# Small expert blocks: the first product in column halves, with TensorE's loop code at another offset and fewer row copies

## The chip, the cores and the metric

The kernel runs on one core of one Trainium2 chip. The metric is device microseconds of one execution, as the median of several runs; lower is better. A core has five engines with queues of their own: TensorE (PE in the profile, with its weight loads as PEld), VectorE (DVE), ScalarE (ACT), GpSimd (POOL) and SyncE (SP), which here issues most DMAs.

## What is computed

Sigmoid attention over 8 batches, 12 heads, 448 positions and 64 columns a head, all in float32, and then a mixture of 8 experts over the 3584 rows of 768 that attention leaves. Cut to what matters:

```python
def _moe_ref(x, w_skip, w_gate, w1, w2):          # x: 3584 x 768
    skip_score = x @ w_skip
    do_compute = skip_score > 0
    out = x.copy()
    xc = x[do_compute]
    logits = xc @ w_gate                          # 8 experts
    e_idx = np.argmax(logits, axis=1)
    ...                                           # gate_w: softmax weight of the chosen expert
    for e in range(E):
        mask = e_idx == e
        h = np.maximum(xc[mask] @ w1[e], 0.0)     # w1[e]: 768 x 1024
        y[mask] = gate_w[mask, None] * (h @ w2[e])  # w2[e]: 1024 x 768
    out[do_compute] = xc + y
    return out
```

## The kernel before, in words

**Attention** takes the first 272 us or so. Each batch's rows are routed as soon as its attention is done: every row that is computed gets a record (its gate and its row number) in a list of its expert. Attention's output is stored to the result, and the experts add to it.

**Two blocks of 128 rows** of the largest expert are then written out by hand, while VectorE plans the rest: a table `slots` says block by block which rows come, what kind of block it is, and which expert's weights are to be loaded behind it.

**The loop** at line 1553 runs over the rest of the blocks, 14 of them here. `choose` reads one word of `slots` and takes one of four arms:

- `FULL` and `SPLIT` (function `block`): 128 rows. Weights and rows are split into a high and a low part (`wh`, `wl`, `xh`, `xl`, type fp32r), and each product is the sum of three. `SPLIT` also makes the split weights of the next expert on ScalarE and VectorE.
- `HALF`: up to 64 rows, plain float32 weights as they were loaded (`raw1`, `raw2`), the array in two column groups of 64 (`side`).
- `FEW`: up to 32 rows, plain float32, four column groups of 32 (`quarter`).

`HALF` and `FEW` are the small blocks, and both have the same parts. The rows lie turned (columns of the row on the partitions) in `xf`, one piece of 128 for each j in range(6). The **first product** multiplies them with `raw1`, 768 x 1024, and leaves its result in PSUM: in `FEW` the 1024 columns lie as four groups of 256 on 32 partitions each, in `HALF` as two of 512 on 64. **relu** copies it to `hs` (ScalarE; two pieces of 128 columns in `FEW`, pieces of 128, 128 and 256 in `HALF`). TensorE **turns** `hs` piece by piece against the identity into PSUM, ScalarE copies the turned pieces to `ht`, and the **second product** multiplies `ht` with `raw2` into `py`. In `FEW` its terms go in the order j = 0, 2, 1, 3, and piece j % 2 of `ht` is what a term needs: the first half of the terms needs the first piece alone.

Between the first product and the turns of `hs`, TensorE also turns the next block's rows (`turn_x`, six turns of 128 x 128 into `pxt`), SP gets the four loads of the next expert's `raw1` (`load_w1`), and POOL the row gather for the block after the next (`fetch`). Behind the turns of `hs`, `ready_x` makes `xh` (`hi_x`, ScalarE), `xf` (`whole_x`, ScalarE: 64 of each 128 columns) and `xl` (`lo_x`, VectorE). `put` scatters the block's result to the output by a DMA on POOL that adds.

The order of the instructions on each engine is the order in the code (`tc.manual_schedule()`); waits between engines are put in by the framework, from what each instruction writes and reads. `ph`, `py` and `pht` are PSUM tiles that all arms share. `ph[0]`, `ph[1]`, `pht[0]` and `pht[1]` are four banks.

[...]

Of the kernel before, what the change touches and what calls it, by code (L numbers as in the profile page):

```python
# [14 lines left out]
AF = mybir.ActivationFunctionType  # L15
# [4 lines left out]
P = 128  # L20
# [3 lines left out]
def kernel(  # L24
# [11 lines left out]
    nc = tc.nc  # L36
# [11 lines left out]
    NK1 = DM // P  # L48
    NK2 = FF // P
    H1 = FF // 2  # L50
# [6 lines left out]
    SM = 32  # L57
# [15 lines left out]
    ident = const.tile([P, P], F32, name="ident")  # L73
# [613 lines left out]
    for n, (b, hp) in enumerate(steps):  # L687
# [39 lines left out]
        for c in range(4):  # L727
            at = wk.tile([P, 2, S], F32, tag="A", name=f"at_{b}_{hp}_{c}", bufs=5)
# [125 lines left out]
    ph = new_ph(0)  # L854
# [13 lines left out]
    xf = rows_pool.tile([P, NK1, MD], F32, name="xf")  # L868
    ys = rows_pool.tile([P, DM], F32, name="ys")
    ht = rows_pool.tile([P, 4 * P], F32, name="ht")  # L870
    hs = rows_pool.tile([P, FF], F32, name="hs")
# [202 lines left out]
    ph = new_ph(1)  # L1074
# [38 lines left out]
    def whole_x(h, pieces):  # L1113
        for s in pieces:
            n = s.stop - s.start
            nc.scalar.activation(
                xf[:, 3 * h + s.start : 3 * h + s.stop, :],
                pxt[h][:, s.start * P : s.stop * P].rearrange(
                    "p (j t) -> p j t", j=n
                )[:, :, :MD],  # L1120
                AF.Copy,
            )

    def ready_x():
        for h in range(2):
            hi_x(h, pxt[h], xh)
        for h in range(2):
            whole_x(h, [slice(j, j + 1) for j in range(3)])
        for h in range(2):
            lo_x(h, pxt[h], xh, xl)  # L1130

# [23 lines left out]
    for j in range(2):  # L1155
        gemm2(j, hh0, hl0, py)
    turn0(1)
    nc.tensor.addr_align(bass.FETCH_BLOCK_INSTRUCTIONS, offset=0, max_nops=0)
    for j in range(2, NK2 - 3):
        gemm2(j, hh0, hl0, py)  # L1160
    pxt = [ps_b.tile([P, 512], F32, tag="b", name="pxt0"), new_t("pxt1")]
# [1 line left out]
        turn_x(xc, h, pxt[h])  # L1163
        hi_x(h, pxt[h], xh)
    for h in range(2):
        whole_x(h, [slice(j, j + 1) for j in range(3)])
    for h in range(2):
        lo_x(h, pxt[h], xh, xl)
    for j in range(NK2 - 3, NK2):
# [52 lines left out]
    raw1 = [[raw1g[h, i // 3][:, i % 3, :] for h in range(2)] for i in range(NK1)]  # L1222
    raw2 = [raw2g[j // 2][:, j % 2, :] for j in range(NK2)]

    ph = [new_t(f"ph{h}") for h in range(2)]
    py = new_s("py")
    pht2 = new_s("pht")
    pht = [pht2[:, h, :] for h in range(2)]

    def next_expert(word):  # L1230
        return word & (NE - 1), (word & (2 * NE)) >> (2 * NE).bit_length() - 1
# [176 lines left out]
    def few(i, word):  # L1408

        nx = next_expert(word)  # L1410
        for o in range(2):
            nc.vector.tensor_copy(gate2[o * SM : (o + 1) * SM], recs[:SM, 0, 0:1])  # L1412
        take_rec()

        def quarter(dst, g, n, a, w, j, most):
            nc.tensor.matmul(  # L1416
                dst[g * SM : (g + 1) * SM, :n],
                a,
                w,
                start=(j == 0),  # L1420
                stop=(j == most - 1),
                tile_position=(0, g * SM),
            )

        Q1 = FF // 4
        for j in range(NK1):
            for g in range(4):
                s = slice((g % 2) * Q1, (g % 2 + 1) * Q1)
                quarter(ph[0], g, Q1, xf[:, j, :SM], raw1[j][g // 2][:, s], j, NK1)
        turned = (pht[0], ph[1])  # L1430
        parts = [slice(c * P, (c + 1) * P) for c in range(2)]
        for s in parts:
            nc.scalar.activation(hs[:, s], ph[0][:, s], AF.Relu)
        for h in range(2):
            for g in range(2):
                load_w1(g, h, nx)
        for h in range(2):
            turn_x(xn, h, pxt[h])
        fetch()
        ht4 = ht[:, : 8 * SM].rearrange("p (c g t) -> p c g t", c=2, g=4)  # L1440
        for s, p in zip(parts, turned):
            nc.tensor.transpose(p[:, :P], hs[:, s], ident)
        for s, p in zip(parts, turned):
            nc.scalar.activation(ht[:, s], p[:, :P], AF.Copy)
        ready_x()
        shift(dve)

        for n, j in enumerate((0, 2, 1, 3)):
            for g in range(4):
                h, o = g // 2, g % 2  # L1450
                m = j + h * (NK2 // 2)
                quarter(
                    py[:, 0, :],
                    g,
                    H2,
                    ht4[:, j % 2, 2 * h + j // 2, :],
                    raw2[m][:, o * H2 : (o + 1) * H2],
                    n,
                    NK2 // 2,
                )  # L1460
        for g in range(4):
            load_w2(g, nx)
        nc.scalar.activation(yh, py[MD:, 0, :H2], AF.Copy, scale=gate2)
        nc.vector.scalar_tensor_tensor(yt, py[:MD, 0, :H2], gate2, yh, op0=ALU.mult, op1=ALU.add)
        put(SM)
        advance()

    def half(i, word):

        nx = next_expert(word)  # L1470
        take_rec()

        def side(dst, g, n, a, w, j, most):
            nc.tensor.matmul(  # L1474
                dst[g * MD : (g + 1) * MD, :n],
                a,
                w,
                start=(j == 0),
                stop=(j == most - 1),
                tile_position=(0, g * MD),  # L1480
            )

        for j in range(NK1):
            for h in range(2):
                side(ph[0], h, H1, xf[:, j, :], raw1[j][h], j, NK1)
        turned = (pht[0], ph[1])
        parts = [slice(0, 2 * P), slice(2 * P, 4 * P)]
        for s in (slice(0, P), slice(P, 2 * P), parts[1]):
            nc.scalar.activation(hs[:, s], ph[0][:, s], AF.Relu)
        for h in range(2):  # L1490
            for g in range(2):
                load_w1(g, h, nx)
        for h in range(2):
            turn_x(xn, h, pxt[h])
        fetch()
        for c in range(4):
            nc.tensor.transpose(
                turned[c // 2][:, (c % 2) * P : (c % 2 + 1) * P],
                hs[:, c * P : (c + 1) * P],
                ident,  # L1500
            )
        for s, p in zip(parts, turned):
            nc.scalar.activation(ht[:, s], p[:, : 2 * P], AF.Copy)
        ready_x()
        shift(dve)

        ht8 = ht.rearrange("p (c h t) -> p c h t", c=4, h=2)
        for n in range(NK2):
            c, h = divmod(n, 2)
            m = h * (NK2 // 2) + c  # L1510
            for o in range(2):
                side(
                    py[:, 0, :],
                    o,
                    H2,
                    ht8[:, c, h, :],
                    raw2[m][:, o * H2 : (o + 1) * H2],
                    n,
                    NK2,
                )  # L1520
        for g in range(4):
            load_w2(g, nx)
        for o in range(2):
            s = slice(o * H2, (o + 1) * H2)
            weigh_sum(ys[:MD, s], py[o * MD : (o + 1) * MD, 0, :H2], recs[:MD, 0, 0:1])
        put(MD)
        advance()
# [56 lines left out]
```

## Time and profile before

| | |
|---|---|
| median of 3 runs | 514.2 us (513.92 to 514.32) |
| the profiled execution's own time | 514.12 us |
| its span, first to last instruction | 512.4 us |
| around the span | 1.7 us |
| mean granted TensorE clock | 0.993 |
| small blocks in the loop | 2 `HALF`, 5 `FEW`, between 7 blocks of 128 rows |

The views that are used: the page with its chain of work that ended last, the timeline (rows are start, duration, engine, line, operation, output<-inputs, shape and count, and in brackets the idle time of the engine before it and what ended it), the table by stretches of time, the list of waits, and the view of one line of code with all its instructions. Times in the timeline are us from the start of the span. Each float32 product is recorded as two matmuls, so 24 calls of `quarter` are 48 records. A matmul's record is longer than its share of TensorE, as matmuls overlap: what one costs is read from where the next one starts.

### The profile page before, as it was taken

The page shows a single profiled execution, that of the slowest core. Times are in us where ns is not written, and L with a number is a line of the kernel's source. Part 1 is how long each engine was busy: PE and PEld are TensorE (multiplying, and loading weights), DVE is VectorE, ACT ScalarE, POOL GpSimd, SP SyncE. Part 2 cuts the span into 40 slices and gives each one's busy share as a digit, 9 for nine tenths or more (in the row PEclk, how much of TensorE's full clock was granted, in tenths as well). Part 3 has the DMA queues.
Part 4 walks back from the last instruction along what each step waited for, and adds up shares of the span by engine and source line. Part 5 has one row for each costly group of instructions (what it writes and reads, how often), then busy time and mean ns, then how long its engine had stood idle before and what let it go on. Part 6 is the DMA issues. An engine that isn't in the chain of part 4 may idle for free. (4 is left out here: it accounts for less than half of the span.)

```text
span 512.4 us, 15271 instructions
## 1 busy us (share of the span) xinstructions
PE 499.9 (98%) x4982; PEld 335.9 (66%) x4983; DVE 294.5 (57%) x745; ACT 271.8 (53%) x480; POOL 258.8 (51%) x405
## 2 busy tenths in 40 slices
PE   8999999999999999999999999999999999999992
PEld 5665555555555555555557988948678787878781
DVE  5565756647868688687785842962132222249432
ACT  5776776767667677677664212933212323259322
POOL 5523455443565786657775341444223434347644
PEclk9999999999999999999999999999999999999997
DMA  7799586677698977897845035979393969697953
GB/s 231 189 235 257 144 205 158 151 172 210 168 240 235 234 198 200 214 261 193 216 99 110 2 95 166 367 226 333 90 373 119 312 246 309 253 315 254 329 214 50
DMA packets 139716, 107.27 MB, mean 209 GB/s; under 512 B 96263, under 2 KB 112265, under 8 KB 139664
## 3 DMA queue, kind: packets, MB, share of 16 engines
q1 hardware_dynamic: 133264, 97.66, 64.5%
q0 software_dynamic: 4736, 8.66, 7.0%
q8 instruction: 33, 0.54, 0.4%
q10 hardware_dynamic: 1664, 0.26, 0.3%
q14 instruction: 19, 0.16, 0.1%
HBM read 98.49 MB, written 17.60 MB: 227 GB/s over the span
## 5 line engine op out<-in xcount | busy, mean ns | idle before, releaser
L256 ACT ACTIVATE at<-s,bias 128x896 f32<-128x896 f32 (+1 forms) x191 | 170.8, 914 | 77.7 <-PE s L236 76.8
L264 PE MATMUL pa<-at,v 64*64 64x448 f32 (+1 forms) x1528 | 161.8, 490 | 0.0
L236 PE MATMUL s<-x 64*64 64x448 f32 (+1 forms) x1504 | 160.6, 494 | 0.3 <-DVE x L216 0.2
L180 POOL COPY kq<-kq 32x896 f32<-32x896 f32 (+1 forms) x96 | 88.0, 917 | 83.7 <-DMA kq<-in_q_dram 41.2
L236 PEld LDWEIGHTS s<-x 64*64 64x64 f32 x1504 | 78.0, 191 | 52.1 <-ACT at L256 20.4
L264 PEld LDWEIGHTS pa<-at,v 64*64 64x64 f32 x1528 | 61.0, 133 | 55.7 <-issue 46.9
L216 DVE STREAM_TRANSPOSE x<-kq 128x448 f32<-128x448 f32 x94 | 82.0, 946 | 4.2 <-POOL kq L180 4.2
L274 DVE TENSOR_TENSOR xt<-xt,pa 128x448 f32<-128x448 f32 x48 | 29.7, 620 | 60.8 <-ACT xt L684 59.5
L486 POOL TENSOR_TENSOR wl<-wr,wh 128x384 fp32r<-128x384 f32 (+1 forms) x28 | 31.3, 1123 | 21.1 <-DVE wh L485 18.9
L413 POOL DMA_INDIRECT lst<-rec,idx x32 | 32.5, 1016 | 13.8 <-DVE nf L923 6.0
L525 ACT ACTIVATE hs<-ph 128x512 f32<-128x512 f32 x14 | 8.4, 598 | 45.9 <-PE ph L516 38.0
L279 DVE STREAM_TRANSPOSE y<-xt 128x448 f32<-128x448 f32 x48 | 31.0, 645 | 1.7
L547 PE MATMUL py<-wh,hh 128*128 128x384 f32 x112 | 31.2, 349 | 0.0
L547 PE MATMUL py<-wl,hh 128*128 128x384 f32 x112 | 29.9, 338 | 0.0
L547 PE MATMUL py<-wh,hl 128*128 128x384 f32 x112 | 29.8, 337 | 0.0
L536 DVE TENSOR_TENSOR hl<-pht,hh 128x512 fp32r<-128x512 f32 x14 | 9.7, 690 | 33.5 <-ACT hh L535 32.2
L516 PE MATMUL ph<-wl,xh 128*128 128x512 f32 x84 | 26.6, 403 | 0.0
L684 ACT ACTIVATE xt<-pa 128x448 f32<-128x448 f32 x48 | 25.7, 536 | 1.2 <-PE pa L264 1.2
L516 PE MATMUL ph<-wh,xh 128*128 128x512 f32 x84 | 25.7, 403 | 0.0
L1349 DVE TENSOR_SCALAR ys<-py,recs 128x384 f32<-128x384 f32 (+1 forms) x18 | 10.4, 612 | 26.0 <-PE py L547 20.8
L502 DVE TENSOR_TENSOR xl<-pxt,xh 128x384 fp32r<-128x384 f32 x30 | 15.3, 552 | 16.5 <-issue 6.5
L516 PE MATMUL ph<-wh,xl 128*128 128x512 f32 x84 | 24.4, 395 | 0.0
(292 smaller groups left out, 683.5 us busy)
## 6 DMA issues: line engine op xcount, KB each, us to landing
raw<-in_moe_w_dram SPq DMA_DIRECT2D x64, 768.0 KB
v<-in_v_dram SPq DMA_DIRECT2D x47, 256.0 KB
out_dram<-y SPq DMA_DIRECT2D x192, 56.0 KB
kq<-in_k_dram SPq DMA_DIRECT2D x23, 448.0 KB
kq<-in_q_dram SPq DMA_DIRECT2D x23, 448.0 KB
wr<-in_moe_w_dram SPq DMA_DIRECT2D x12, 256.0 KB
wr<-in_moe_w_dram SPq DMA_DIRECT2D x16, 192.0 KB
lst<-fill SPq DMA_DIRECT2D x4, 464.0 KB
```

The lines of the kernel that those rows point to most:

```text
L180: nc.gpsimd.tensor_copy(a[to, :, :, :BT], a[at, :, :, BT:])
L216: nc.vector.transpose(xs[:, n].rearrange("p (r j) -> p j r", j=NJ), t.rearrange("p (j d) -> p j d", d=D)[:, :, :BT],)
L236: nc.tensor.matmul(sc[m * D : (m + 1) * D, j, : qs.stop - qs.start], xs[r, 0, first::NR7], xs[r, 1, qs], start=True, stop=True,)
L256: nc.scalar.activation(at[:, :, :n], sc[:, :, :n], AF.Sigmoid, bias=bias, scale=SCALE)
L264: nc.tensor.matmul(pa[j * D : (j + 1) * D, r, qs], vt[r][j][:, c if r == j else (c + 1) % NV, :], at[rs, j, : qs.stop - qs.start], start=( ...
L274: nc.vector.tensor_tensor(x, x, pa[:, 1, :S], op=ALU.add)
L279: nc.vector.transpose(y, xts[b][:, hp, :])
L413: put = nc.gpsimd.indirect_dma_start(out=lst[:, :], out_offset=bass.IndirectOffsetOnAxis(ap=idx[:, c : c + 1], axis=0), in_=rec[:, c, :], ...
L486: nc.gpsimd.tensor_tensor(lo, r, hi, op=ALU.subtract)
L516: nc.tensor.matmul(ph[h], a[:, j * P : (j + 1) * P], w[j][h], start=(n == 0), stop=(n == len(t) - 1),)
L547: last = nc.tensor.matmul(py[:, o, :H2], a[h][:, js], w[j][:, o * H2 : (o + 1) * H2], start=(j == 0 and n == 0), stop=(j == NK2 - 1 and n ...
L684: nc.scalar.activation(xts[b][:, hp, :], pa[:, 0, :S], AF.Copy)
```

## The change

In both small blocks the first product is made in two halves of its columns, one behind the other, into two banks (`ph[0]`, `ph[1]`), and each half has its relu right behind it. The turn of the first half and its copy come ahead of the loads and of `turn_x`; the turn of the second half and its copy stay behind `fetch()`. The turned halves go to `pht[0]` and `pht[1]` (before: `pht[0]` and `ph[1]`). The number of matmuls of the first product doubles, each with half of the columns. `whole_x` makes `xf` in one copy of three pieces for each half of the row, where it made three; the loop of `SPLIT` had that already. The offset of TensorE's loop code goes from 0 to 188.

```diff
@@ ready_x, and the first rows ahead of the loop @@
         for h in range(2):
-            whole_x(h, [slice(j, j + 1) for j in range(3)])
+            whole_x(h, (slice(0, 3),))
@@ ahead of the loop @@
     turn0(1)
-    nc.tensor.addr_align(bass.FETCH_BLOCK_INSTRUCTIONS, offset=0, max_nops=0)
+    nc.tensor.addr_align(bass.FETCH_BLOCK_INSTRUCTIONS, offset=188, max_nops=0)
@@ few @@
         Q1 = FF // 4
-        for j in range(NK1):
-            for g in range(4):
-                s = slice((g % 2) * Q1, (g % 2 + 1) * Q1)
-                quarter(ph[0], g, Q1, xf[:, j, :SM], raw1[j][g // 2][:, s], j, NK1)
-        turned = (pht[0], ph[1])
+        turned = pht
         parts = [slice(c * P, (c + 1) * P) for c in range(2)]
-        for s in parts:
-            nc.scalar.activation(hs[:, s], ph[0][:, s], AF.Relu)
+        for c, s in enumerate(parts):
+            for j in range(NK1):
+                for g in range(4):
+                    at = (g % 2) * Q1 + c * P
+                    quarter(ph[c], g, P, xf[:, j, :SM], raw1[j][g // 2][:, at : at + P], j, NK1)
+            nc.scalar.activation(hs[:, s], ph[c][:, :P], AF.Relu)
+        ht4 = ht[:, : 8 * SM].rearrange("p (c g t) -> p c g t", c=2, g=4)
+
+        def turn_part(c):
+            nc.tensor.transpose(turned[c][:, :P], hs[:, parts[c]], ident)
+            nc.scalar.activation(ht[:, parts[c]], turned[c][:, :P], AF.Copy)
+
+        turn_part(0)
         for h in range(2):
             for g in range(2):
                 load_w1(g, h, nx)
         for h in range(2):
             turn_x(xn, h, pxt[h])
         fetch()
-        ht4 = ht[:, : 8 * SM].rearrange("p (c g t) -> p c g t", c=2, g=4)
-        for s, p in zip(parts, turned):
-            nc.tensor.transpose(p[:, :P], hs[:, s], ident)
-        for s, p in zip(parts, turned):
-            nc.scalar.activation(ht[:, s], p[:, :P], AF.Copy)
+        turn_part(1)
         ready_x()
@@ half @@
-        for j in range(NK1):
-            for h in range(2):
-                side(ph[0], h, H1, xf[:, j, :], raw1[j][h], j, NK1)
-        turned = (pht[0], ph[1])
+        def turn_part(h):
+            for c in range(2):
+                s = slice(c * P, (c + 1) * P)
+                nc.tensor.transpose(turned[h][:, s], hs[:, parts[h]][:, s], ident)
+            nc.scalar.activation(ht[:, parts[h]], turned[h][:, : 2 * P], AF.Copy)
+
+        turned = pht
         parts = [slice(0, 2 * P), slice(2 * P, 4 * P)]
-        for s in (slice(0, P), slice(P, 2 * P), parts[1]):
-            nc.scalar.activation(hs[:, s], ph[0][:, s], AF.Relu)
+        for s, one, pieces in zip(parts, ph, ((slice(0, P), slice(P, 2 * P)), (slice(0, 2 * P),))):
+            for j in range(NK1):
+                for h in range(2):
+                    side(one, h, 2 * P, xf[:, j, :], raw1[j][h][:, s], j, NK1)
+            for p in pieces:
+                nc.scalar.activation(hs[:, s][:, p], one[:, p], AF.Relu)
+        turn_part(0)
         ...
         fetch()
-        for c in range(4):
-            nc.tensor.transpose(
-                turned[c // 2][:, (c % 2) * P : (c % 2 + 1) * P],
-                hs[:, c * P : (c + 1) * P],
-                ident,
-            )
-        for s, p in zip(parts, turned):
-            nc.scalar.activation(ht[:, s], p[:, : 2 * P], AF.Copy)
+        turn_part(1)
         ready_x()
```

More of the change, by code (lines that the diff above doesn't have):

```diff
@@ L1165 @@
     for h in range(2):
-        whole_x(h, [slice(j, j + 1) for j in range(3)])
+        whole_x(h, (slice(0, 3),))
     for h in range(2):
```

## The prediction

> **What bounds the kernel now.** I read the page first, for the engine that carries the span and its chain.
>
> ```profile
> span 512.4 us, 15271 instructions
> PE 499.9 (98%) x4982; PEld 335.9 (66%) x4983; DVE 294.5 (57%) x745; ACT 271.8 (53%) x480; POOL 258.8 (51%) x405
> q8 instruction: 33, 0.54, 0.4%
> ```
>
> TensorE is busy for 98% of the span, and the other engines for little more than half. A gain must therefore be time in which TensorE does nothing useful, or idles. The change touches only the small blocks, so I next read TensorE's timeline of one `FEW`, and beside it ScalarE's and VectorE's rows of the same microseconds.
>
> ```profile
> 419.36 2.80 PE L1416 MATMUL ph<-raw,xf 128*32 128x256 f32 x48
> 422.08 0.88 PE L492 MATMUL pxt<-ident,xn 128*128 128x128 f32 x6
> 422.80 0.30 PE L1442 MATMUL pht<-ident,hs 128*128 128x128 f32 x1
> 423.02 0.30 PE L1442 MATMUL ph<-ident,hs 128*128 128x128 f32 x1
> 423.51 2.90 PE L1416 MATMUL py<-raw,ht 128*32 128x384 f32 x32 [0.19 <-DVE gate L1412]
> 426.34 0.97 PE L516 MATMUL ph<-wh,xh 128*128 128x512 f32 x3
> ...
> 422.38 0.45 ACT L1433 ACTIVATE hs<-ph 128x128 f32<-128x128 f32 x2 [8.11 <-PE ph L1416]
> 423.14 0.28 ACT L1444 ACTIVATE ht<-pht 128x128 f32<-128x128 f32 x1 [0.31 <-PE pht L1442]
> ...
> 423.16 0.31 DVE L1412 COPY gate<-recs 32x1 f32<-32x1 f32 x2 [1.91 <-ACT hs L1433]
> ```
>
> A `FEW` takes 426.34 - 419.36 = 6.98 us. Between the turns of `hs` (422.80) and the second product (423.51) lie 0.71 us for two turns, and the six turns of rows before them took 422.80 - 422.08 = 0.72, 0.12 each. So 0.71 - 0.24 = 0.47 us are not work: the second turn came 0.22 behind the first, and then the array stood still.
>
> The row names VectorE's `gate` as the releaser of the second product. I don't believe it. The first copy to `ht` ends at 423.14 + 0.28 = 423.42, 0.09 ahead of the product; and the fourth `FEW` tells the two apart:
>
> ```profile
> 474.63 2.77 PE L1416 MATMUL py<-raw,ht 128*32 128x384 f32 x30 [0.19 <-ACT ht L1444]
> ...
> 477.04 0.31 DVE L1412 COPY gate<-recs 32x1 f32<-32x1 f32 x2
> ```
>
> There `gate` came 2.4 us after the second product had started, with the same 0.19 of idle time, now put down to ScalarE. The product waits for the copy, and so for turn, copy and relu in a row behind the end of the first product. That is the wait at which the change aims. `HALF` has the same gap:
>
> ```profile
> 363.03 5.37 PE L1474 MATMUL ph<-raw,xf 128*64 128x512 f32 x24
> 368.33 0.88 PE L492 MATMUL pxt<-ident,xn 128*128 128x128 f32 x6
> 369.04 0.38 PE L1497 MATMUL pht<-ident,hs 128*128 128x128 f32 x2
> 369.42 0.41 PE L1497 MATMUL ph<-ident,hs 128*128 128x128 f32 x2
> 369.94 5.38 PE L1474 MATMUL py<-raw,ht 128*64 128x384 f32 x32
> 375.25 0.97 PE L516 MATMUL ph<-wh,xh 128*128 128x512 f32 x3
> ...
> 368.56 0.72 ACT L1489 ACTIVATE hs<-ph 128x128 f32<-128x128 f32 x3 [10.62 <-PE ph L1474]
> 369.46 0.38 ACT L1503 ACTIVATE ht<-pht 128x256 f32<-128x256 f32 x1 [0.18 <-PE pht L1497]
> ```
>
> **The first product in halves.** It has the same columns in twice as many matmuls: 96 records of 128 columns for 48 of 256 in `FEW`, 48 of 256 for 24 of 512 in `HALF`. Does a matmul cost something beside its columns? The logits are the nearest row, float32 with 32-column weights in four groups, 112 columns:
>
> ```profile
> 273.96 0.87 PE L492 MATMUL b_px<-ident,x 128*128 128x128 f32 x6
> 274.77 1.36 PE L296 MATMUL pl_last<-xt,wcat 128*32 128x112 f32 x48
> 276.06 1.65 PE L516 MATMUL b_ph<-wh,b 128*128 128x512 f32 x6
> ```
>
> They take 276.06 - 274.77 = 1.29 us for 48 records. With four groups at once that is 48 x 28 = 1344 columns; the first product of `FEW` takes 422.08 - 419.36 = 2.72 for 48 x 64 = 3072. The difference gives 1.43 / 1728 = 0.83 ns a column, and leaves 1.29 - 1.12 = 0.17 us that don't go with columns. If this is the change of the array's shape, once per product, the halves are free. If it goes with records, 48 more cost 0.17 again. `HALF` leans to the former: its products have the same columns in 24 records (368.33 - 363.03 = 5.30) and in 32 (375.25 - 369.94 = 5.31). So eight records more cost 0.01, 24 more 0.03. I take 0.03 in both blocks, with 0 and 0.17 as ends in `FEW`.
>
> [...]
>
> **The turns.** In `FEW` behind the first product come now: turn of the first half, six turns of rows, turn of the second half: 8 x 0.12 = 0.96 us. The relu of the first half, 0.28 us at most, runs under the second half's 1.3 us; its copy (0.28) lies under the row turns (0.72), behind the second relu, which it shares ScalarE with: relu ends about 422.38 + 0.28 = 422.66, copy about 422.95. The turn of the second half is due at 422.08 + 7 x 0.12 = 422.92, and its relu is done 0.26 before. Nothing is waited for, until the second product changes the array's shape: turns to logits cost 274.77 - 273.96 - 0.72 = 0.09 for that. The second piece of `ht` is needed only half-way through the second product (1.4 us later). So the second product would start at 422.08 + 0.96 + 0.09 = 423.13, not 423.51: 0.38 gained. From this go 0.03 (above) and 0.05 for one semaphore instruction of TensorE's queue between the last turn and the product, which had been hidden under the wait (the row gives least, median and longest time in ns, and the first and last start in us):
>
> ```profile
> L1416 PEld LDWEIGHTS ph<-raw,xf x240: 106/110/111, 393.8 to 498.2; 128*32 128x32 f32 x120
> ...
> L1416 PEldq EVENT_SEMAPHORE  x80: 51/51/214, 392.4 to 500.5; - x80
> ```
>
> That is 0.30 for each `FEW`; without the wait hidden at all it is 0.38, and with the record cost and several such instructions in the open (three, 0.15) 0.06.
>
> `HALF`: ten turns of 0.12 and the change of shape, 368.33 + 1.20 + 0.09 = 369.62, not 369.94; less 0.03 is 0.29, and I take 0.30. Its second relu is one copy of 256 columns, which at the 0.38 of such a copy ends at 368.94; its turn is due at 369.3.
>
> **Which blocks count.** Five `FEW` and two `HALF` stand in the loop, and behind each of them but the last a block of 128 rows starts at once on TensorE (375.25, 426.34). The last one is different: POOL has the end.
>
> ```profile
> 505.30 0.19 POOL L1322 TENSOR_TENSOR jk<-yt 64x2 f32<-64x2 f32 x1
> 506.02 1.49 POOL L574 DMA_INDIRECT out_dram<-yt,rh  x1 [0.53 <-issue]
> ...
> 503.76 0.61 DVE L1464 SCALAR_TENSOR_TENSOR yt<-py,gate,yh 64x384 f32<-64x384 f32 x1 [0.75 <-ACT yh L1463]
> ```
>
> `yt`, the block's result, is done at 504.37, and POOL reaches the instruction that needs it at 505.30, from work of its own. The chain puts the gather before it down to the product (`xn` behind `py`), but POOL idles just as long ahead of it whatever is named:
>
> ```profile
>   PE py L1416: 3.0, 4
>   PE pht L530: 2.9, 4
>   PE py L547: 2.2, 3
>   PE py L1474: 1.5, 2
> ```
>
> 0.73 to 0.75 each: its own preparation. So the last `FEW` gives nothing, and the sum is 4 x 0.30 + 2 x 0.30 = 1.8 us.
>
> **Fewer row copies.** Six copies of 64 columns become two of 192 in `ready_x`:
>
> ```profile
> 424.34 0.81 ACT L1116 ACTIVATE xf<-pxt 128x64 f32<-128x64 f32 x6
> 465.35 0.54 ACT L1116 ACTIVATE xf<-pxt 128x192 f32<-128x192 f32 x2
> ```
>
> 0.27 us of ScalarE, off the path: the six end at 425.15, and TensorE takes up the next block at 426.34 without idling. What is behind them, `xl` on VectorE, can only come sooner. I cost it at nothing; if ScalarE's idle time around it were gone, it would be 0.27 gained.
>
> **Weight loads.** The first of four `load_w1` waits till its rows of `raw1` are read. That was half-way through the first product, and is now three quarters: 0.68 us later in `FEW`, 1.3 in `HALF`. The loads are followed on SP's queue by the other seven. Only `SPLIT` behind a `FEW` uses the weights soon, at 456.97, 9.6 us after the first issue:
>
> ```profile
> 447.34 3.73 SPq L1234 DMA_DIRECT2D raw<-in_moe_w_dram  x4
> ...
> 456.97 1.66 ACT L1252 ACTIVATE wh<-raw 128x512 fp32r<-128x512 f32 x3
> L1252 ACT ACTIVATE wh<-raw 128x512 fp32r<-128x512 f32 x12 | 6.7, 623 | 0.0
> ```
>
> ScalarE never idles ahead of them, so the landing has slack that the row doesn't size: between 0 and 0.68 + 0.3 = 1.0 us once. I take 0.
>
> **The code's offset.** It changes no operation. TensorE's wait at the loop's head is what it can touch, and no block of code later shows a stall.
>
> ```profile
> PEld ph L516 <- DVEq L1553: 0.3, 1, 0.3
> ```
>
> The gain is at most these 0.3. The price of code not there in time is one packet of q8: 0.4% of 16 x 512.4 us over 33 is 1.0 us. I take 0.
>
> **The sum.** The profiled execution took 514.12 us, 0.08 below the median of 514.2. 514.1 - 1.8 = **512.3 us**. About 0.2%, 1.0 us, is what a measurement of this kernel can tell from no change.
>
> **Rivals.**
>
> *Half of the gain* (512.9 to 513.8): TensorE's queue takes its semaphores one at a time, and behind the second turn several stand between it and the product. At 0.06 to 0.2 a block it would be 0.3 to 1.2 us. For it speaks that the second turn came 0.22 behind the first though the two relu pieces were only 0.45 - 0.28 = 0.17 apart; against, that 0.09 sufficed between the copy's end and the product. Chance 0.18.
>
> *More than forecast* (511.0 to 511.6): 0.38 in all seven blocks, which would need the last to count, is 2.7; with the loop's head 3.0. POOL's rows speak against it. Chance 0.06.
>
> *Slower, by code fetches* (515 to 521): one mechanism, in TensorE's queue. [...] Code not held costs 1.0 us a fetch. TensorE's queue enters a block 1.4 us ahead of the array (the semaphores start at 392.4, the matmuls at 393.8), so one fetch a block hides and a second shows 0.6; in 14 blocks that is 8.4, less 1.8, 521 at most. From two fetches a block it decides; at the loop's head alone it is 1.0 once. Against it: 33 packets for some 10,000 records of TensorE, and equal gaps at all blocks. [...] Chance 0.08.
>
> *Narrow matmuls cost their weight loads* (518 to 522): a load of 110 ns no longer hides under four matmuls of 107, so 24 groups of four show 0.11 where 12 did. That is 1.3 us a `FEW`, 5.2 over four, less 1.8. [...] The logits, at 112 columns and 27 ns a record, speak against it. Chance 0.03.
>
> *Forecast* (511.7 to 512.8): 0.65.
>
> **How the numbers follow.** Faster needs more than 1.0 us: the forecast, the rival of more, and a small part of the half gain, 0.65 + 0.06 + 0.03 = 0.74. Same is the rest of the half gain, 0.15. Slower is 0.08 + 0.03 = 0.11. The range goes from 511.5 to 513.8: it leaves out the slower rivals (0.11) and most of the rival of more.
>
> **What would show it.** In each `FEW`: 96 records of `ph`, 2.7 us; one turn of `hs`, six of rows, one of `hs`; the second product 3.8 us behind the start of the first, not 4.15; 6.7 us for the block. `HALF` 11.9, not 12.2. The idle time at the second product falls from 0.19 to under 0.1. The prediction is wrong if the first product takes over 2.9 us in `FEW`, if the second product still waits for a copy of `ht`, if the last block moves the end, or if blocks start later behind the one before them.

## The result, and the profile after

| | before | after |
|---|---|---|
| median of 13 runs each, one series | 514.62 us (513.92 to 515.33) | 518.43 us (516.86 to 522.89) |
| ratio after / before | | 1.0078 (95% interval 1.0063 to 1.0093) |
| the profiled execution: own time, span | 514.12, 512.4 us | 520.39, 518.7 us |

The changed kernel is 3.8 us slower; 512.3 was forecast. All ratios below are to the kernel before, run in the same series on the same chip. That matters, because one condition differs between the series: in some of them before takes 514.4 us, in others 520, with the same chip in both kinds (number 14 gave 519.92 in one series and 514.38 in another). What differs is looked at below; kernels are compared within a series.

The page of after: span and busy time by engine, the granted clock in 40 slices, the code fetches.

```profile
span 518.7 us, 15626 instructions
PE 500.1 (96%) x5270; PEld 349.0 (67%) x5271; DVE 295.2 (57%) x745; ACT 269.0 (52%) x428; POOL 255.2 (49%) x405
PEclk9999999999999999999999999999999999998997
q8 instruction: 33, 0.54, 0.4%
```

TensorE is busy as long as before (499.9 then), in a longer span: most of the loss is idle time, 2% more of the span. The digit 8 in the fourth slice from the end is new. The list of TensorE's waits (us in total, times, longest) names the idle time:

```profile
PE ph L1416 <- ACT wh L1258: 2.0, 1, 2.0
PE ph L1477 <- ACT wh L1258: 1.6, 1, 1.6
PE pa L264 <- DMA v<-in_v_dram: 1.3, 1, 1.3
PE ph L516 <- issue: 1.2, 1, 1.2
```

Two first products of small blocks wait for `wh`, the split weights that only `SPLIT` makes and that no small block reads. The load of `v` lies in the attention part; it is 0.2 in the next profile of the same kernel. The fourth is the loop's first product, waiting for TensorE's own queue.

A `FEW` behind a `FULL`, on TensorE and ScalarE, to set beside the 6.98 us of before:

```profile
422.64 2.83 PE L1416 MATMUL ph<-raw,xf 128*32 128x128 f32 x96
425.39 0.33 PE L1437 MATMUL pht<-ident,hs 128*128 128x128 f32 x1
425.56 0.82 PE L492 MATMUL pxt<-ident,xn 128*128 128x128 f32 x6
426.22 0.33 PE L1437 MATMUL pht<-ident,hs 128*128 128x128 f32 x1
426.48 2.84 PE L1416 MATMUL py<-raw,ht 128*32 128x384 f32 x32
429.24 0.98 PE L516 MATMUL ph<-wh,xh 128*128 128x512 f32 x3
...
425.72 0.28 ACT L1433 ACTIVATE hs<-ph 128x128 f32<-128x128 f32 x1 [1.06 <-PE pht L1437]
```

The 96 narrow records take 425.39 - 422.64 = 2.75 us against 2.72 for 48 wide ones, the second product starts 3.84 behind the first, and the block takes 429.24 - 422.64 = 6.60 us. Here the halves do what they were meant to. The `FEW` behind the second `SPLIT` looks otherwise:

```profile
472.67 0.34 PE L547 MATMUL py<-wh,hl 128*128 128x384 f32 x1
475.04 4.61 PE L1416 MATMUL ph<-raw,xf 128*32 128x128 f32 x96 [2.03 <-ACT wh L1258]
479.58 0.33 PE L1437 MATMUL pht<-ident,hs 128*128 128x128 f32 x1
...
470.48 3.08 ACT L1258 ACTIVATE wh<-raw 128x768 fp32r<-128x768 f32 x4
473.94 1.58 ACT L1258 ACTIVATE wh<-raw 128x768 fp32r<-128x768 f32 x2 [0.39 <-SPq L1552]
```

The product starts at 475.04. `SPLIT` makes eight of these copies, two ahead of the six shown, so the seventh is the first of the last row. Alone on the timeline it reads:

```profile
473.94 0.85 ACT L1258 ACTIVATE wh<-raw 128x768 fp32r<-128x768 f32 x1 [0.39 <-SPq L1552]
```

It ends at 473.94 + 0.85 = 474.79, and in the trace TensorE's queue passes its wait for ScalarE at 474.83, 0.04 behind it. The 0.39 us of idle time ahead of this copy end when the last load of `raw2` lands, at 473.84. Then the product takes 4.54 us for 2.75. The table by stretches shows why (the number ahead of the DMA share is the granted clock):

```profile
475.40:478.80 3.40, 3.40 (x76) 3.40 (x70) 3.03 (x7) 0.40 (x2) 1.73 (x2) 0.51 0.00 0
```

The granted clock was 0.51 for 3.4 us, right behind 2.03 us of idle time. That explains the digit 8, and 1.7 us more.

### The profile page after: what moved, and what is told of

The parts are those of the page before. It is cut to its first block, busy times and chain, and to the rows that moved or that the text cites. A ratio compares the mean times of both kernels' runs of the same rounds, so it can differ in the third digit from the quotient of the medians.

```text
span 518.7 us, 15626 instructions
## 1 busy us (share of the span) xinstructions
PE 500.1 (96%) x5270; PEld 349.0 (67%) x5271; DVE 295.2 (57%) x745; ACT 269.0 (52%) x428; POOL 255.2 (49%) x405
## 5 line engine op out<-in xcount | busy, mean ns | idle before, releaser
L264 PE MATMUL pa<-at,v 64*64 64x448 f32 (+1 forms) x1528 | 167.5, 490 | 1.3 <-DMA v<-in_v_dram 1.3
L236 PE MATMUL s<-x 64*64 64x448 f32 (+1 forms) x1504 | 165.3, 494 | 0.1
L236 PEld LDWEIGHTS s<-x 64*64 64x64 f32 x1504 | 82.2, 191 | 48.8 <-issue 20.4
L264 PEld LDWEIGHTS pa<-at,v 64*64 64x64 f32 x1528 | 64.7, 133 | 55.5 <-issue 46.4
L502 DVE TENSOR_TENSOR xl<-pxt,xh 128x384 fp32r<-128x384 f32 x30 | 15.3, 553 | 17.2 <-PE py L1477 7.4
```

What stands on the lines that cost most here:

```text
L236: nc.tensor.matmul(sc[m * D : (m + 1) * D, j, : qs.stop - qs.start], xs[r, 0, first::NR7], xs[r, 1, qs], start=True, stop=True,)
L264: nc.tensor.matmul(pa[j * D : (j + 1) * D, r, qs], vt[r][j][:, c if r == j else (c + 1) % NV, :], at[rs, j, : qs.stop - qs.start], start=( ...
```

## Where the time went, block by block

`p_before` and `p_after` are the two kernels again, in one series.

p_before: 

> The kernel before once more, so that its profile comes from the same chip as the next three. Every theory expects the shape of its first profile: no wait of TensorE for ScalarE's weight copies of more than 0.5 us at the head of a small block behind a SPLIT block, no stretch at half clock in the loop, loop branches under 1 us. If blocks for few tokens take about 7.5 us here too (they took 7.0 in the first profile of before and 7.5 in the six-copies kernel), that length belongs to the chip and not to the change.

p_after: 

> The changed kernel as it is, on this chip. Count theory (a small block's TensorE waits for a count of ScalarE that the arm with the fewest instructions behind the row copies fixes): waits for wh of 1.6 and 2.0 us again behind the two SPLIT blocks, about 4 us over before. If blocks for few tokens gain 0.1 us instead of 0.4, the whole is 5 to 8 us over before. Rival (the code offset alone is at fault): no difference to the first profile either, but the kernel with the offset alone is then as slow as this one.

Before took 514.50 us there, after 517.89, ratio 1.0071 (1.0052 to 1.0090); the two profiled spans are 512.5 and 514.5. From the starts of the blocks' first products on the timeline (us):

| | p_before | p_after | difference |
|---|---|---|---|
| start of the loop | 313.64 | 314.24 | +0.60 |
| first `SPLIT` | 18.70 | 20.19 | +1.49 |
| two `HALF` | 12.23, 12.26 | 12.01, 11.93 | -0.55 |
| three `FEW` behind `FULL` | 6.99, 6.99, 6.99 | 6.56, 6.58, 6.58 | -1.25 |
| second `SPLIT` | 18.54 | 20.66 | +2.12 |
| `FEW` behind it | 7.10 | 6.73 | -0.37 |
| last `FULL` | 18.63 | 18.56 | -0.07 |
| last `FEW` and the end | 16.31 | 16.31 | 0 |

The other `FULL` blocks agree within 0.02. The sum is +1.97, the spans differ by 1.98. The start of the loop holds a difference of the attention too: counted from the last logits, at 274.80 and 274.48, it comes 38.84 and 39.77 us later, so the queue costs 0.93 there. So the gain is there, 2.2 us in all, and two waits behind `SPLIT` (3.6) and the loop's start (0.6) take more than it. This execution had no half clock (granted 1.00 from 472.9 to 479.6, behind the longer wait); others, like the one above, pay 1.7 us on top, which fits the wider spread of after.

## The experiments

**Theories.** *Count*: a small block's TensorE must wait until the row copies to `xf` of the block before are done. Any arm may have been that block, so one wait has to serve them all: it asks for a count of ScalarE's instructions, set back from the end of the block by as many as follow the copy in the arm where the fewest do. With six copies five more follow the first; with two only one does. In `SPLIT`, where the rows' copies stand ahead of eight weight copies, TensorE then waits for the seventh of them. The count itself isn't in the profile; the wait's end is. *Rival, code*: the offset of 188, or the longer code, costs the time.

**e1 to e4**, one series; before took 519.92 us. Each has one part undone, or one alone.

```diff
 e1   whole_x(h, (slice(0, 3),))  ->  whole_x(h, [slice(j, j + 1) for j in range(3)])   (both places)
 e2   offset=188  ->  offset=0
 e3   both of these: the halves alone
 e4   before, with whole_x(h, (slice(0, 3),)) in both places
```

e1: 

> The changed kernel with the row copies put back to six, offset 188 kept. Theory 'count': the small block behind a SPLIT waits for a count of ScalarE's instructions that is set by how many follow the row copy in the shortest arm; with two copies that count is reached only with SPLIT's seventh wh copy (waits of 1.6 and 2.0 us in the changed profile), with six it is reached by the third. Then both waits are gone, the slow clock behind the second with them, and the time is about 514 us: the kernel before, less 2 us for the halves, plus 1.2 us at the loop's head. Rival 'bank': the waits come from the halves, which write a second bank; then they stay and the time is about 518.

e2: 

> The changed kernel with offset 0, two copies kept. Theory 'head': offset 188 makes TensorE's first jump into SPLIT's code wait for a fetch (a branch of 2.0 us, 1.2 us idle); with offset 0 this is gone and the time is about 517.2 us, with the two waits behind SPLIT unchanged. Rival: the stall comes from the longer code whatever the offset; then the idle 1.2 us stay and the time is about 518.4.

e3: 

> The column halves alone: six copies and offset 0. By 'count' and 'head' together about 512.7 us, the time that was predicted for the whole change; FEW about 6.6 us and HALF 11.9 us. By 'bank' over 516 us, with the waits behind SPLIT. If the longer code stalls at the loop's head at any offset, about 514 us.

e4: 

> The kernel before with two row copies in place of six and nothing else. By 'count' the small blocks behind the two SPLITs wait 1.6 to 2 us each, and the clock falls behind the longer one in some runs: 518 to 520 us. By 'bank' no change, 514.6 us.

| | time | ratio (95%) |
|---|---|---|
| e1, six copies, 188 | 521.50 | 1.0033 (1.0019 to 1.0047) |
| e2, two copies, 0 | 527.80 | 1.0166 (1.0146 to 1.0185) |
| e3, six copies, 0 | 526.58 | 1.0125 (1.0101 to 1.0149) |
| e4, before with two copies | 526.57 | 1.0123 (1.0101 to 1.0145) |

e4 has neither the halves nor the offset, and it loses 6.6 us. Its waits:

```profile
PE ph L1474 <- ACT wh L1258: 2.9, 1, 2.9
...
PE ph L1416 <- ACT wh L1258: 1.6, 1, 1.6
```

The first is followed by 3.4 us at half clock (granted 0.50), and its `HALF` takes 14.09 instead of 12.2. So fewer copies alone make the waits, and here the half clock followed one of them. Against `p_before_2` (below; another series at the same level of before) the first `SPLIT` is 2.9 us longer, its `HALF` 1.9 and the second `SPLIT` 1.7: 6.5 in all, and the loss is 6.6. Of the first wait 1.06 us is ScalarE itself waiting for a load of `raw2` ahead of its seventh copy; in `p_before_2` it stands still 1.19 us at the same place, and TensorE doesn't wait. In e1, with six, the wait behind the second `SPLIT` shrinks to this (TensorE, then ScalarE):

```profile
474.56 1.91 PE L1416 MATMUL ph<-raw,xf 128*32 128x128 f32 x40
476.78 1.74 PE L1416 MATMUL ph<-raw,xf 128*32 128x128 f32 x56 [0.31 <-ACT wh L1258]
...
472.10 4.53 ACT L1258 ACTIVATE wh<-raw 128x768 fp32r<-128x768 f32 x6
```

What is left fits the count too: the sixth copy has nothing behind it, so the sixth piece of rows (records 41 to 48 of the first half) waits for the very last weight copy, 472.10 + 4.53 = 476.63, and goes on at 476.78. The whole-width product came to its sixth piece after 2.2 us, when that copy was all but done; the half comes to it after 1.2. The first `HALF` waits piece by piece too, 0.5 us the longest, and takes 13.12 us for 12.2. So e1 is still 0.3% slower than before, where its theory had it a little faster.

e2 and e3 were a surprise. The old offset was expected to be harmless, and it costs about 5 us, stretches of 3.4 us at half clock included (granted 0.50 and 0.52 in e2). e2's start of the loop and first `HALF`, and from the view of one line the branch there (least, median and longest in ns, first and last start):

```profile
317.43 0.76 PE L516 MATMUL ph<-wh,xh 128*128 128x512 f32 x1 [2.20 <-issue]
340.38 7.18 PE L1477 MATMUL ph<-raw,xf 128*64 128x256 f32 x48 [2.81 <-ACT wh L1258]
```

```profile
L1552 PEldq COMPARE_BRANCH  x8: 73/204/3987, 314.2 to 478.0; - x8
```

The branch took 3.1 us at 314.2, going into the first `SPLIT`, and 4.0 us at 334.3, leaving it; the second is what the row at 340.38 puts down to `wh`. e3 has the same two, 3.2 and 4.0. From e1 to e3, which differ in the offset alone, it is 5.1 us. So 188 is no loss against 0: with the longer code it is the better of the two. It is TensorE's queue that stalls, at a branch: these four stand against 0.20 us for the median one in both runs.

**e5 and e6**, in the series of `p_before` and `p_after`, aim at the two causes one by one.

```diff
 e5   ready_x:  whole_x(0), whole_x(1), hi_x(0), hi_x(1), lo_x    (before: hi_x, hi_x, whole_x, whole_x, lo_x)
 e6   before, with offset=0 -> offset=188
```

e5: 

> The changed kernel, still with two row copies, but issued ahead of the two hi parts in ready_x instead of behind them, so that three ScalarE instructions instead of one follow the first copy, and two the second, in every arm. Count theory: the count is then reached with the third or fourth ScalarE instruction behind SPLIT's own row copies, some 2 to 3 us sooner than with its last weight copy; the waits of 1.6 and 2.0 us for wh fall below 0.3 and the stretch at half clock goes: 4 to 6 us faster than the changed kernel, within 1.5 us of before on either side. Rival (two wide copies are late by their own length, 0.4 us more each before the rows are there): the waits stay at 1 us or more, and the kernel at most 1 us faster than the changed one. Rival (code fetch is the cost): nothing moves, since TensorE's code is the same.

e6: 

> The kernel before, with the code offset of 188 alone. Count theory: none of its waits returns, six copies are kept. If an offset is good or bad only with the code it stands before (the six-copies kernel lost 5 us at offset 0 and nothing at 188), this one, with shorter code, can lose: a branch of 2 to 4 us at the first entry of an arm, 0 to 5 us slower than before. If the offset of 188 is a gain by itself, 0.3 to 1 us faster than before and the branch at the loop's head shorter than in before.

e5 took 515.22 us, 1.0018 (1.0004 to 1.0032): still two copies, and 2.7 us less than after (4 to 6 were forecast). Both waits for `wh` are gone; only the order on ScalarE was changed. With that the rival that wide copies come late by their own length falls, and the trace shows the count move: two more instructions follow each copy, and TensorE's queue passes its wait behind the second `SPLIT` two weight copies sooner, at 470.33, 0.04 behind the fifth (470.29). In `after`, `p_after` and e4 it was 0.04 behind the seventh. The `FEW` there takes 6.72 us, 0.38 less than in `p_before`. The order has its own price, by the same rule: now the `hi` parts stand last, and the `FULL` behind the fourth `FEW` waits for all of ScalarE (second row). The first row is the loop's start, which stays late:

```profile
314.96 0.47 PE L516 MATMUL ph<-wh,xh 128*128 128x512 f32 x1 [1.26 <-issue]
...
478.93 0.94 PE L516 MATMUL ph<-wh,xh 128*128 128x512 f32 x3 [0.71 <-ACT yh L1466]
```

From the last logits to the loop e5 takes 40.30 us for 38.84 in `p_before`. These 1.5 us are twice what it loses in all, so e5's order with a loop that starts in time might come out ahead of before; that kernel wasn't run.

e6 took 515.21 us, 1.0012 (1.0001 to 1.0022). The branch at its loop's head took 1.67 us, in `p_before` 0.24 at most; the line's view of e6, then of `p_before`:

```profile
L1548 PEldq COMPARE_BRANCH  x8: 73/195/1667, 313.4 to 468.7; - x8
```

```profile
L1548 PEldq COMPARE_BRANCH  x8: 73/194/235, 312.7 to 467.3; - x8
```

So 188 is a small loss with the short code, and 0 a large one with the long code: what counts is how the offset and the length of the code go together. The page's queue for instructions, q8, took 0.54 MB in 33 packets, 16 KB each.

**Theory of the fetch**, from these rows: at a long branch TensorE's queue waits for a packet of its code, and where the code lies decides whether it must. The packets' starts speak for it: in `after` the branch ended at 316.15, 2.50 us behind the start of a packet on q8 at 313.65, and in `p_after`, e1 and e5 too it ended 2.5 to 2.7 us behind one. Which instructions a packet holds, no trace shows, so what is forecast below for each offset is an estimate. In e1 the branch took 0.70 us and the array none of it: its loop starts 38.88 us behind the last logits, 38.84 in `p_before`. The loop's first block is a `SPLIT`, whose code, counted in the program, stood 390 instructions behind the dispatch before and 427 to 435 after, behind the longer `HALF`.

**e7 to e10**, another series; before took 520.06 us.

```diff
 e7    offset=188 -> offset=226
 e8    ready_x:  whole_x(0, (slice(0, 3),)), hi_x(0), hi_x(1), whole_x(1, three pieces), lo_x
 e9    both
 e10   e1 (six copies, old order) with offset=226
```

e7: 

> The changed kernel with its code offset at 226 instead of 188, nothing else. [...] The waits of 1.6 and 2.0 us for wh stay. Time: 1 to 1.5 us under the changed kernel, 1.5 to 3 over before. Rival (188 has nothing to do with the late start; the longer code has): the branch keeps its 2 us and the time stays.

e8: 

> The changed kernel at its offset of 188, with ready_x in another order: the first half's wide copy ahead of the two hi parts, the second half's three narrow copies behind them (four copies in all, five ScalarE instructions behind the first, three behind the second hi part). Count theory: the waits for wh behind SPLIT go, as with both copies ahead; the wait of 0.7 us for yh in the FULL block behind the last FEW, and the 0.14 us more in each FULL block, which came when the hi parts were ScalarE's last, go too. 1 to 1.5 us faster than with both copies ahead, 0 to 1 us faster than before; the late start of the loop stays. Rival (the 0.7 us came from VectorE's late gate and not from the order): it stays, and the time is that of both copies ahead.

e9: 

> Both repairs in one: that order of ready_x and offset 226. If both theories hold, nothing is left but the gain of the halves, 0.41 us in each of four FEW blocks and 0.2 and 0.3 in the two HALF blocks: 1.6 to 2.3 us faster than before where FEW blocks take 7.0 us in before, about 0.5 us of FEW's gain less where they take 7.5. If the two costs share a cause, less than 1 us faster.

e10: 

> The changed kernel with the six row copies of before, at offset 226: the halves alone without either cost. Count and fetch theory: 1.3 to 2.3 us faster than before, within 0.5 us of the kernel with both repairs. If fewer copies are a gain by themselves, that one is faster than this by 0.5 us or more.

| | time | ratio (95%) |
|---|---|---|
| e7 | 524.13 | 1.0075 (1.0051 to 1.0100) |
| e8 | 521.75 | 1.0022 (1.0009 to 1.0036) |
| e9 | 521.26 | 1.0025 (1.0010 to 1.0039) |
| e10 | 524.92 | 1.0085 (1.0059 to 1.0111) |

In e7 the branch no longer stalls (0.25 us at most), against the rival, and the waits stay (1.9 and 1.5 us); in e8 the waits go (0.3 left) and the branch stays at 2.27 us. The theories had each repair's effect right, but not the times: e7 came 4.1 us over before for 1.5 to 3, as half clock followed its first wait (1.93 us; granted 0.62 in a window of 3.4 us behind it), and e8 1.7 over where level to 1 under was forecast. And e9 and e10, which have neither cost, are no faster than before. Their first `SPLIT`, first e9, then e10:

```profile
318.93 0.39 PE L516 MATMUL ph<-wl,xh 128*128 128x512 f32 x1 [0.72 <-issue]
```

```profile
319.50 0.47 PE L516 MATMUL ph<-wh,xl 128*128 128x512 f32 x1 [1.22 <-issue]
```

The stall has moved into `SPLIT`, a few products in. e10 also has a tail of 20.49 us against 17.3 to 17.5 in its neighbours: a packet on q8 starts at 520.67, and TensorE's part of the end comes 2.4 behind that, some 3 us late.

**e11 and e12** try another place, with both kernels' profiles in the same series; before took 520.25 us.

```diff
 e11   e9 with offset=204
 e12   e10 with offset=204
```

p_before_2: 

> The kernel before, for its profile on this chip. If this chip runs before in about 520 us: FEW blocks of 7.5 to 7.7 us and a tail of 17 us in this kernel too (the longer blocks belong to the chip); rival (the halves lengthen the blocks there): 7.0 us. If it runs before in about 514.5 us: 7.0 us again by both.

p_after_2: 

> The changed kernel, for its profile on this chip: waits for wh of 1.6 and 2.0 us behind the SPLIT blocks and a branch of about 2 us at the loop's head again, 2 to 7 us over before.

e11: 

> One copy ahead, three behind the hi parts, as in the kernel with both repairs, but at offset 204. [...] Fetch theory: no branch over 0.5 us, no idle over 0.3 us in the first block, no longer tail: the first SPLIT block takes 18.6 us. 0.7 us faster than at 226; against before 1.6 to 2.3 us faster where FEW takes 7.0 us in before, 0 to 1 us faster where before takes 520. Rival (226 lost its gain for another reason): the same time as at 226, 0.2% over before.

e12: 

> The six row copies of before with the halves, at offset 204. [...] Fetch theory: the 1.2 us of idle time in the first block and the 3 us in the tail, which this kernel had at 226, both go, some 4 us faster than there; within 0.5 us of the kernel with one copy ahead. Rival (six copies are slow with the halves for a reason of their own): more than 1 us slower than that one.

e11 took 523.46 us, 1.0066 (1.0050 to 1.0081), e12 522.93, 1.0052 (1.0032 to 1.0071): a miss, both expected at or under before. The tail is cured in e12 (17.48), but e11 stalls twice, and e12 as well (1.20 and 2.04):

```profile
317.15 0.47 PE L516 MATMUL ph<-wh,xh 128*128 128x512 f32 x1 [1.34 <-issue]
...
322.13 0.40 PE L516 MATMUL ph<-wl,xh 128*128 128x512 f32 x1 [1.25 <-issue]
```

The first comes from the dispatch's other branch (2.2 us at 314.5), which ends at 316.7, 2.4 us behind the start of a packet on q8 at 314.3. Why it is this branch at 204 and not the one that stalls at 188 is not shown.

`p_before_2` shows what differs in the series where before takes 520. Its `FEW`, with ScalarE's relu first:

```profile
427.51 0.45 ACT L1433 ACTIVATE hs<-ph 128x128 f32<-128x128 f32 x2 [8.75 <-PE pxt L492]
...
423.85 2.80 PE L1416 MATMUL ph<-raw,xf 128*32 128x256 f32 x48
426.58 0.87 PE L492 MATMUL pxt<-ident,xn 128*128 128x128 f32 x6
427.94 0.30 PE L1442 MATMUL pht<-ident,hs 128*128 128x128 f32 x1 [0.48 <-ACT hs L1433]
```

The product ends at 426.58 and its relu starts at 427.51, 0.93 us later; in `p_before` these are 422.19 and 422.48, 0.29. A `FEW` takes 7.63 us here, in the kernel before, and 7.50 to 7.55 in `p_after_2`: of the halves' gain of 0.42 about 0.1 is left. The loop also starts 3.9 us later (317.50 for 313.64); 3.8 of that is there at the last logits already (278.62 for 274.80), so it is the attention's. What the relu waits for is TensorE's own signal: in `p_before` the semaphore updates of the product's last four matmuls come 0.04 apart, at 422.25 to 422.38; here the first comes at 426.64 and the next only at 427.32. Why is open. The attention, three `FEW` (0.64 each) and the end (17.3 us for 16.3) come to 6.7 us; the two spans differ by 6.5.

**e13 and e14**, in a series where before took 514.38 us.

```diff
 e13   before, with the FEW part of the change alone (six copies, offset 0, HALF as before)
 e14   e9 with offset=222
```

e13: 

> The kernel before with the FEW part of the change alone: offset 0, six row copies, HALF blocks as before. Both theories: no branch over 0.5 us, no wait for wh over 0.3 us, no stretch at half clock. Where before takes about 514.5 us, the FEW blocks fall from 7.0 to 6.6 us: 1.2 to 1.7 us faster. Where before takes about 520, they fall from 7.63 to 7.51 and the one behind the second SPLIT block rises from 7.03 to 7.85: 0.3 us faster to 0.8 slower. Rival (a third cost sits in the halves themselves): 1 us slower than before or more on either chip.

e14: 

> Both halves, one copy ahead and three behind the hi parts, offset 222. [...] Fetch theory: branch under 0.5 us, an idle time of 0.2 to 0.7 us in the first SPLIT block, which takes 18.8 to 19.3 us; the same as at 226 to 0.4 us faster. [...]

e14 took 514.65 us, 1.0003 (0.9991 to 1.0014), as the fetch theory had it: branches under 0.4 us, 0.3 us idle in the first `SPLIT`, which takes 19.13. So both halves, without the long waits and with little left of the stall, come out level with before. Counted from the last logits, which come 0.8 us later than in `p_before`, its execution is 0.2 us shorter: the second `HALF` and the three `FEW` behind `FULL` gain 1.54 us (the first `HALF` nothing), 0.43 go back in the first `SPLIT`, and 0.93 in the `FEW` behind the second, which takes 8.03 for 7.10. Its product, and ScalarE's last two weight copies of `SPLIT`:

```profile
470.31 1.42 PE L1416 MATMUL ph<-raw,xf 128*32 128x128 f32 x32
472.20 0.43 PE L1416 MATMUL ph<-raw,xf 128*32 128x128 f32 x8 [0.47 <-ACT wh L1258]
472.93 1.74 PE L1416 MATMUL ph<-raw,xf 128*32 128x128 f32 x56 [0.31 <-ACT wh L1258]
...
471.30 1.58 ACT L1258 ACTIVATE wh<-raw 128x768 fp32r<-128x768 f32 x2 [0.36 <-SPq L1552]
```

e13 took 514.34 us, 0.9997 (0.9987 to 1.0008), and misses the 1.2 us that it was to gain, though its copies and offset are those of before. Against `p_before` (another series at the same level), e13's three `FEW` behind `FULL` gain 0.34 to 0.36 each, 1.05 together. The `FEW` behind the second `SPLIT` gives 0.56 back, and the `FULL` behind that 0.24 more (18.87 for 18.63), in pieces of at most 0.15 that I can't assign; start and first `SPLIT` differ by 0.14; the last `FEW` takes 0.4 less and the end stays at 16.32 behind its start. The sum, -0.11, is the difference of the spans, 512.44 and 512.55. The fourth `FEW`:

```profile
469.59 1.94 PE L1416 MATMUL ph<-raw,xf 128*32 128x128 f32 x40
471.84 1.74 PE L1416 MATMUL ph<-raw,xf 128*32 128x128 f32 x56 [0.31 <-ACT wh L1258]
```

Forty records that take 1.15 us elsewhere (40/96 of 2.75) take 2.25, idle time included: piece by piece of the rows they wait for ScalarE's count behind the weight copies, the last of which ends at 471.69. The six copies were just enough for a product that comes to its last piece after 2.2 us, and aren't for one that comes to it after 1.2.

No kernel here beats before by more than can be told.

## Why the prediction was wrong, point by point

- **What bounds the kernel, and the gap that the halves close: right.** The second product of `FEW` starts 3.84 us behind the first for 4.15: 0.31, and 0.30 was forecast. `FEW` as a whole gains 0.41 to 0.43 in `p_after`; some 0.07 more is in the second product itself (2.76 us for 2.83 in the rows of after and before), which the sum didn't have. `HALF` gains 0.22 and 0.33 (0.30). Narrow records cost 0.03 us, as taken: 2.75 for 2.72. In the series at 520 us `FEW` gains 0.1.
- **The last `FEW` gives nothing: right.** 16.31 us to the end before and after.
- **"Fewer row copies": the step that failed.** It was costed at nothing, because six copies end 1.2 us ahead of the next block. That looked at the copies' time behind `FEW` and not at the wait on them, which the edit moves in every arm, behind `SPLIT` above all. Measured: 1.5 and 2.1 us in `p_after`, 1.7 more where the clock halves, 6.6 us for this edit alone in e4. The sign of the result comes from this step. The prediction's own sign, blocks that start later behind the one before them, is what came; but no rival held it. That 518.4 lies within two of them (code fetches, 515 to 521, and narrow matmuls, 518 to 522) is luck: most of the loss isn't fetches, and the narrow matmuls cost 0.03.
- **"The code's offset": too small.** Costed at 0, with 1.0 as the price of a fetch at the loop's head. The stall there, 1.6 to 2.3 us in the queue (`p_after`, `after`, e5, e8), shows as 0.8 to 1.5 us of idle time on the array. The rival of code fetches had the right place, and its price of 1.0 once at the loop's head is about what the array saw; that price was an estimate, a packet's time on q8, and in `after` the queue went on 2.50 us behind the packet's start. Repeated fetches in the loop didn't come: in `after` the median of the eight branches at that line is 0.20 us, and q8 has no packet from 329.5 to 517.5. What wasn't seen is that a good offset for the short code need not be one for the longer. Of the offsets tried with the longer code only 188 in e1 costs nothing. The idle time put down to TensorE's own queue is 2.2 and 2.3 us at 0 (e2, e3, where the branch of 4.0 us is put down to `wh`), 1.2 to 1.8 at 188 (`after`, e5, e8), 2.6 and 3.2 at 204 (e11, e12), 0.3 at 222 (e14), and 0.3, 0.7 and 1.2 at 226 (e7, e9, e10). Why each offset has its time is not shown.
- **The `FEW` behind `SPLIT`** was counted like the others. With six copies, or with three of them narrow, its gain of 0.30 turns into a loss: with the half, the last rows are wanted before ScalarE has finished `SPLIT`'s weights (7.84 us in e1, 7.66 in e13, 8.03 in e14). Only e5, with both copies ahead, has the gain there (6.72), and there its order makes the `FULL` behind wait 0.7 us.
- **The weight loads** on SP later: 0 was taken of 0 to 1.0 us, and the landing was looked for at `raw1`. It shows at `raw2`: the last load lands 19.5 us behind the start of the second `SPLIT` in `after`, `p_after` and e14, for 17.2 to 17.9 in `before`, `p_before` and e6, and ScalarE waits 0.4 us for it ahead of the seventh copy. That is 0.4 of the 2.1 above. In e5 it lands at 18.2, and nothing waits.

## What to carry to other kernels

When an edit changes how many instructions follow a write on its engine, look at every wait on that write, in every branch that can come before it, and not only at how long the writes take: a count that serves several arms is fixed by the shortest of them. Work that is asked for sooner loses the cover it had, so a gain counted in one place must be counted again behind each kind of neighbour. And after any change in the length of looped code, read the branches at the loop's first entry; an offset that was good for the old length says nothing about the new. Here 0, with branches of 0.24 us at most in `p_before`, cost 5.1 us with the longer code (e3 against e1).

## What the runs showed of the hardware

- **Half clock after short idle times.** Of ten stretches of 1.9 to 2.9 us in which TensorE stood still, seven were followed by a window of 3.4 us at about half clock: granted 0.51 in `after`, 0.50 and 0.52 in e2, 0.50 in e3 and e4, 0.53 in e12, and 0.62 in e7. Three were followed by a clock of 1.00 (`p_after`, `p_after_2`, e3's second). The length doesn't tell them apart: 1.93 us (e7), 2.03 (`after`) and 2.04 (e12) were followed by half clock, 2.1 (`p_after`), 2.3 (`p_after_2`) and 2.8 (e3's second) not. What does is not shown. In `after` the 2.03 us of idle time and the slow product behind it (4.54 us for 2.75) cost 3.8 together.
- **The stall can come inside `SPLIT`.** In e9 to e12 the array stood still inside the first `SPLIT`, for 0.72, 1.22, 1.25 and 2.04 us, each until 2.2 to 2.7 us behind the start of a packet on q8.
- **Two levels of the same kernel.** With the same kernel, 514.4 or 520 us came for whole series; the longer one has relu 0.6 us later behind its product in each `FEW` that follows a `FULL`, as TensorE's signal comes late, and an attention that is 3.8 us longer (`p_before_2`). The cause wasn't found.
